# Carried-state matmuls in 64-row quadrants with a drain, states without zero blocks, stretches of two units and another opening, in a fused retention and ELU feed-forward kernel

## The chip, the cores and the metric

One of the eight cores of one Trainium2 chip runs the whole problem. The metric is the device time of one execution in microseconds (us). The core has five engines that run side by side, each through its own queue in order: TensorE (PE in the profile, its weight loads PEld), VectorE (DVE), ScalarE (ACT), GpSimd (POOL) and SyncE (SP), which here only issues transfers. Transfers run on 16 shared DMA engines.

## The reference

Multi-head retention over q, k, v of shape (8 batches, 8 heads, 576 positions, 64), then a feed-forward layer with an ELU-like function on the 4608 rows of 512:

```python
scores = scale * np.matmul(q, k.transpose(0, 1, 3, 2))
gamma = 1.0 - 2.0 ** (-5.0 - np.arange(H))
rel = pos[:, None] - pos[None, :]
Dmat = np.where(rel >= 0, gamma[:, None, None] ** rel[None, :, :], 0.0)
attn = np.matmul(scores * Dmat[None], v)

x = attn.transpose(0, 2, 1, 3).reshape(B * S, H * D)
h = x @ w_in                                   # 512 -> 2048
g = np.where(h > 0.0, h, np.exp(np.minimum(h, 0.0)) - 1.0)
out = g @ w_out                                # 2048 -> 512
```

## The kernel before

**Retention in chunks of 64.** The decay is split: q is multiplied by gamma to the power of its position and k by the inverse (`scaled`, L475), so that within a chunk of 64 positions a plain triangular mask is left, and all earlier chunks come in through a carried state, the running sum of k^T v per head. A *unit* n is a quarter of the first 512 positions and 8 heads of one batch: n = 4b + 2T + w, with batch b, T = 0 or 1 for the first or second 256 positions, and w for the first or last four heads. The last 64 positions of all batches form two *tails*, units 32 and 33 (t0, t1). Units 0 to 7 are laid out with even and odd positions apart; units 8 to 31 are "far" (`it.far`): positions in order, four chunks x = 0..3 each.

**What one far unit does.** SP loads q, k and v in two transfers each (L394). POOL scales q and k in four pieces and casts v (L475, L510). A DMA transpose (L562) makes qkT. PE then does four things for a unit, by these functions:

- `do_scores`: 16 matmuls of 64 rows by 64, one for each quadrant of the array in turn;
- `do_inter`: the carried states times the queries, into the output's PSUM bank. A state of two heads is kept as a 128x128 matrix with the two 64x64 blocks on the diagonal and zeros beside them, so one 128-row matmul serves both heads. It is 2 x 4 matmuls, and 2 x 3 where T = 0, for the first chunk of a batch has no state;
- `do_values`: 16 matmuls of 64 rows by 64, masked scores times v, added in the same bank;
- `do_state`: 16 matmuls of 64 rows by 64, k^T v of each chunk, into the other half of the same two banks.

`mask_step` (L837) masks the scores on DVE. `after_far` adds the four chunk states up on DVE (L801, L803), and its `emit_b` (L812) makes the block-diagonal form on POOL, from one 128x128 f32 sum to a 128x256 bf16 tile: three `s_mid` and one `s_end` per unit. `put_x` (L882) copies the output to xt on ACT or DVE.

**A stretch.** `stretch(prev, it)` puts one visit of PE to attention together: inter of the unit before, scores of this unit, values of the unit before, state of this unit. There is one stretch for each unit from 5 on, and a last one. It takes two of the six PSUM banks of class f (`SLOTS`), and the score tile sc. Units 0 to 4 are done in the opening by `early` and `early_out`.

**Feed-forward.** Blocks of rows go through `ffn1` (h = x w_in into a bank, exp on ACT L996, then ACT L1006 or DVE L1010, then DVE L1018 or L1020 gives g) and `ffn2` (g w_out into a bank, copied out on ACT L1054, stored by SP L1062). The first three batches make six narrow blocks of 256 rows, the others wide blocks of 512; the tails are a wide block of their own and come ahead of batch 7. F1 of one block alternates with F2 of the one before, in pieces of about 0.87 us on PE.

**Order.** Nothing is ordered by hand. All operations are given to `Plan`, each with a cost per engine that can do it, dependencies, a rank and buffers; `Plan.run` simulates the engines, the DMA queues and the buffers with these costs, always taking the ready operation of least rank, and the kernel emits every engine's instructions in the order that comes out. `FROM` holds the earliest times of the eight weight transfers (w_in then w_out, issued by POOL, L453 and L461), `ON` binds named operations to one engine, `RANKS` shifts named ranks, `FAR_LD`, `FAR_TR` and the `dma=` tuples hold what transfers are taken to cost. Up to 50 us the emitter also fills planned gaps of PE with matmuls on zeros (L268, L1178), so that its clock stays up.

The core of the stretch in the old kernel:

```python
if prev is not None:
    do_inter(prev, xkey)
if it is not None:
    do_scores(it)
if prev is not None:
    do_values(prev, xkey)
if it is not None and not it.tail:
    do_state(it, views)
```

Of the kernel before, what the change touches and what calls it, by code (L numbers as in the profile page):

```python
# [36 lines left out]
class Plan:  # L37
# [30 lines left out]
    def run(self, began):  # L68
# [58 lines left out]
        while len(order) < len(self.ops) or any(wire.values()) or events:  # L127
# [53 lines left out]
            for e, h in heads.items():  # L181
                h[1] -= step * rate[e]
                if h[1] < 1e-6:
                    wire[e].pop(0)
                    lanes[e] -= 1
                    heapq.heappush(events, (now + LEAVE, next(count), h[2]))
# [12 lines left out]
RANKS = {}  # L199
# [8 lines left out]
FROM = (8.96, 10.28, 13.13, 15.23, 17.0, 17.0, 17.44, 17.82)  # L208
ON = {'mid1': 'DVE', 'be2': 'DVE', 'md_1_0': 'ACT', 'xc1_2': 'DVE', 'cv0': 'DVE', 'md_1_1': 'ACT', 'cq12': 'DVE'}
DIRECT = True  # L210
FAR = 8
FAR_LD = 0.64
FAR_TR = 1.9
# [20 lines left out]
def kernel(  # L234
# [145 lines left out]
    def load_main(it, srcs="qkv"):  # L380
        n = it.n
        if not hasattr(it, "ld"):
            it.ld = {}
        for s in srcs:
            src = {"q": q, "k": k, "v": v}[s]
            key, cls = (("rv", n), "rv") if s == "v" else (("rq" + s, n), "rqk")

            away = (s, n) in AWAY

            if it.far:  # L390
                for e in range(2):
                    def emit_far(op, src=src, key=key, e=e):
                        i0 = 2 * P * it.T + e * P
                        pin(nc.sync.dma_start(tiles[key][:, :, e], src[it.b, 4 * it.w : 4 * it.w + 4, i0 : i0 + P, :].rearrange(  # L394
                            "h p d -> p h d")))

                    it.ld[s, e] = chain[0] = add(f"ld{s}{e}_{n}", {"SP": 0.52}, [], emit_far, len(plan.ops),
                                                 take=[] if e else [T(cls, key, [P, 4, 2, D], FP32)],
                                                 use=[key] if e else [], dma=(FAR_LD, 32), after=chain.get(0))
                continue  # L400

            def emit(op, src=src, key=key, away=away):
                dst = tiles[key].rearrange("p h e d -> p h (e d)")
                pin((nc.scalar if away else nc.sync).dma_start(  # L404
                    dst,
                    src[it.b, 4 * it.w : 4 * it.w + 4, 2 * P * it.T : 2 * P * (it.T + 1), :].rearrange(
                        "h (p e) d -> p h (e d)", e=2),
                ))

            take, use, held = [T(cls, key, [P, 4, 2, D], FP32)], [], []  # L410
            if s == "q" and n in HOLD:
                def emit_hold(op, key=key):
                    pin(nc.gpsimd.memset(tiles[key][:, 0, 0, :1], 0.0))

                held.append(add(f"hold{n}", {"POOL": 0.13}, [], emit_hold, -5, take=take))
                holds.append((held[0], HOLD[n]))
                take, use = [], [key]
            it.ld[s] = add(f"ld{s}{n}", {"ACT": 0.5} if away else {"SP": 0.46}, held, emit,
                           -10 ** 6 if away else len(plan.ops), take=take, use=use,
                           dma=(0.9 if n or s != "v" or away else 1.8, 32), after=None if away else chain.get(0))  # L420
            if away:
                it.ld[s].at = AWAY[s, n]
            else:
                chain[0] = it.ld[s]

    def load_tail(it):
# [3 lines left out]
        def load(name, cls, key, rows, src, b, first):  # L430
            def emit(op):
# [3 lines left out]
            chain[0] = add(name, {"SP": 0.46}, [], emit, len(plan.ops),  # L435
                           take=[T(cls, key, [P, H, D], FP32)] if first else [], use=[] if first else [key],
                           dma=(0.8, 32), after=chain.get(0))
# [8 lines left out]

    w_in_ld, w_out_ld = {}, {}

    def load_w_in(n0, n1, after):
# [5 lines left out]
        op = add(f"wi{n0}", {"POOL": 0.8}, [], emit, -1000, dma=(2.62 * (n1 - n0), 32 * (n1 - n0), 4.9), after=after)  # L455
# [3 lines left out]
    def load_w_out(n, after):  # L459
# [4 lines left out]
        w_out_ld[n] = add(f"wo{n}", {"POOL": 0.8}, [], emit, -1000, dma=(2.62, 32, 4.9), after=after)  # L464
# [102 lines left out]
    def prepare_tail(it):  # L567
# [3 lines left out]
        for m in range(2):  # L571
            for j in range(2):
# [14 lines left out]
                def emit_t(op, m=m, j=j):  # L587
# [5 lines left out]
                                     dma=(1.0, 32)))  # L593
# [27 lines left out]
    def do_scores(it):  # L621
        n = it.n
        sc = tiles["sc", n]
# [12 lines left out]
        if it.far:  # L636
            for x in range(4):
                for i in range(2):
                    r = slice(i * D, (i + 1) * D)
                    for c in range(2):  # L640
                        cs = slice(c * C, (c + 1) * C)
                        mm(sc[cs, i, x * C : (x + 1) * C], tt[r, 4 + x, cs], tt[r, x, cs], start=True, stop=True)
# [11 lines left out]
    def do_inter(it, xkey):  # L654
# [10 lines left out]
        if it.far:  # L665
            tt = tiles["qkT", n]
            for x in range(4):
# [4 lines left out]
                for hl in range(2):  # L672
                    acc((xkey, c), 0, 2, tiles[xkey, c][:, hl * P + e * C : hl * P + (e + 1) * C], s[:, hl],
                        tt[:, e * 2 + hl, c * C : (c + 1) * C])
# [114 lines left out]
    def after_far(it, st, views, bank_keys, prev):  # L789
# [3 lines left out]
        for x in range(4):  # L793
# [16 lines left out]

            def emit_b(op, key=key, out=out):
# [6 lines left out]
            blk = add(f"b{x}_{n}", {"POOL": 0.62, "DVE": (0.42, 1.5)}, [run], emit_b, it.rank + 3,  # L818
                      take=[T(name, out, [P, 2, P], BF16)], use=[key])
# [6 lines left out]
    def mask_step(it, sc):  # L826
        n = it.n
        def emit(op):
            if it.tail:
                pin(nc.vector.tensor_tensor(  # L830
                    tiles["pt", n].rearrange("p i h n -> p (i h n)").rearrange("p (x n) -> p x n", n=ST),
                    tiles["sc", n].rearrange("p i n -> p (i n)").rearrange("p (x n) -> p x n", n=ST),
# [3 lines left out]
            if it.far:  # L836
                pin(nc.vector.tensor_tensor(  # L837
                    far_pt(n).rearrange("p (i x) n -> p i x n", i=2),
                    tiles["sc", n][:, :, : 4 * C].rearrange("p i (x n) -> p i x n", n=C),
# [5 lines left out]
                tiles["sc", n].rearrange("p i (h n) -> p (i h) n", h=2),  # L845
# [4 lines left out]
                      take=[T("pt", ("pt", n), [P, 2, 2, 2 * P], BF16)], use=[("sc", n)], banks=[("sc", 0)])  # L850
# [40 lines left out]
    def cost_of(it, parts):  # L891
        t = 0.0
        if it.far:
            return ("i" in parts) * (0.27 + 0.06 * it.T) + 0.1 * sum(x in parts for x in "svt")
# [19 lines left out]
    def stretch(prev, it):  # L914

        xkey = ("x", it.n if it else "last")
        deps, use, take, cost = [], [], [], 0.22
        if prev is not None:
            deps += [prev.mask, *inter_deps(prev)]
            use += inter_uses(prev)  # L920
            cost += cost_of(prev, "iv")
        if it is not None:
            deps += it.turned + ([] if it.tail else [it.cv])
            take.append(T("sc", ("sc", it.n), [P, 2, 512], FP32))
            use += [("qkTt", it.n, m, j) for m in range(2) for j in range(2)] if it.tail else [("qkT", it.n), ("qkn", it.n), ("vn", it.n)]
            cost += cost_of(it, "st")
        views = [((xkey, c), 0, lambda c=c: tiles[xkey, c][:, 2 * P : 4 * P if it.far else 3 * P]) for c in range(2)]

        def emit(op):
            if prev is not None:  # L930
                do_inter(prev, xkey)
            if it is not None:
                do_scores(it)
            if prev is not None:
                do_values(prev, xkey)
            if it is not None and not it.tail:
                do_state(it, views)

        st = add(f"S{it.n if it else 'last'}", {"PE": cost}, deps, emit, (it or prev).rank - 4, take=take, use=use)
        reserve(st, [(xkey, c) for c in range(2)])  # L940
        if it is not None:
            mask_step(it, st)
            if not it.tail:
                after_state(it, st, views, [(xkey, 0), (xkey, 1)])
        if prev is not None:
            put_x(prev, xkey, st)

    def early(it):
        n = it.n
        sc = add(f"sc{n}", {"PE": 0.3}, it.turned, lambda op: do_scores(it), it.rank,  # L950
# [163 lines left out]
    for it in items[:EARLY]:  # L1114
        early(it)
        early_out(it)
    for n in range(4):
        load_w_in(n, n + 1, None)
    prev = None
    for it in items[EARLY:]:  # L1120
        stretch(prev, it)
        prev = it
    stretch(prev, None)
# [93 lines left out]
```

## Time and profile before

| what | value |
|---|---|
| median of 3 runs | 305.57 us (305.03 to 306.04) |
| the profiled execution's own time | 305.64 us |
| its span, first to last instruction | 303.9 us |
| mean granted TensorE clock | 1.000 |
| POOL, state blocks L812 | 72 s_mid 44.5 us busy, 24 s_end 15.6 us |
| PE, carried states of units | 160 s_mid matmuls 10.3 us, 32 s_end 3.8 us |
| HBM read, written | 36.70 MB, 9.44 MB |

The page is of one execution. Busy time of PE counts matmuls that overlap in the pipeline, so what one costs is read from the distance between starts. A group's mean in the page is the time from start to end of one matmul, 0.193 us for one of 64 columns, of which most lies beside its neighbours. Some matmul records are missing (a stretch can look one 512-column matmul longer than it is). "Waits" are idle times of an engine, put down to what came last. The 24 s_end operations of L812 are one per far unit.

### The profile page before, as it was taken

To read this page: it belongs to the slowest core of one execution; us is meant where nothing else is said; L and a number is where in the kernel's file an instruction comes from. 1 tells how busy PE (TensorE), PEld (TensorE's weight loads), DVE (VectorE), ACT (ScalarE), POOL (GpSimd) and SP (SyncE) were. 2 spreads that over 40 slices of the span, in tenths; PEclk is the share of its full clock that TensorE was granted. 3 is DMA by queue.
4 is the path that set the end of the run, shared out by engine and by line. 5 is a ranking of instruction groups with operands and counts; after the bars stand their busy time and mean duration, and the time that the engine had idled before them with its cause. 6 is when DMAs were issued, how large, how long until landed. Compare 5 with 4: busy or idle time off the path is not lost.

```text
span 303.9 us, 8654 instructions
## 1 busy us (share of the span) xinstructions
PE 291.6 (96%) x3378; PEld 169.6 (56%) x3418; DVE 214.2 (70%) x436; ACT 155.2 (51%) x305; POOL 178.4 (59%) x300
## 2 busy tenths in 40 slices
PE   8889999999999999999999999999997999999995
PEld 4768746767666754445554544545444544444444
DVE  5878935958877857996988897788871486666500
ACT  2439724748655546765855544445541583444311
POOL 5880389688989897889889889697532000000000
PEclk9999999999999999999999999999999999999999
DMA  7999998999899999989999999987667101011132
GB/s 206 270 206 210 235 303 218 173 218 187 194 193 232 214 185 204 206 193 183 193 188 224 204 186 199 204 169 171 137 130 168 37 2 36 35 36 37 43 97 71
DMA packets 142010, 50.13 MB, mean 165 GB/s; under 512 B 120720, under 2 KB 137488, under 8 KB 141968
## 3 DMA queue, kind: packets, MB, share of 16 engines
q1 hardware_dynamic: 137744, 45.37, 71.4%
q0 software_dynamic: 4224, 4.19, 8.3%
q8 instruction: 27, 0.44, 0.6%
q14 instruction: 15, 0.12, 0.1%
HBM read 36.70 MB, written 9.44 MB: 152 GB/s over the span
## 4 chain that ended last, share of the span: by engine, by line
PE 85%; DMA 6%; DVE 3%; issue 2%; SPq 1%; POOL 1%; ACT 1%; POOLq 0%; DVEq 0%; ACTq 0%
PE f L268 82%; PE sc L268 3%; DMA rv<-in_v_dram 3%; DMA rqk<-in_q_dram 2%; DMA rqt<-in_k_dram 1%; DVE em L1010 1%; DVE g L1020 1%; DMA qkTt<-qkt 1%; DVE g L1018 1%; SPq L404 1%; PE f L523 0%; ACT e L996 0%; POOL qkn L475 0%; POOL qkt L578 0%; DVE mid L803 0%
## 5 line engine op out<-in xcount | busy, mean ns | idle before, releaser
L268 PE MATMUL f<-xt,w_in_sb 128*128 128x256 bf16 (+1 forms) x755 | 139.8, 325 | 0.8 <-DVE xt L882 0.2
L268 PE MATMUL f<-w_out_sb,g 128*128 128x512 bf16 (+2 forms) x581 | 137.2, 367 | 3.4 <-issue 1.7
L996 ACT ACTIVATE e<-f 128x512 f32<-128x512 f32 x144 | 85.4, 597 | 77.7 <-PE f L268 73.5
L268 PEld LDWEIGHTS <-w_in_sb 128*128 128x128 bf16 x768 | 73.7, 98 | 52.0 <-DVE xt L882 0.5
L268 PEld LDWEIGHTS <-g 128*128 128x128 bf16 x608 | 56.5, 98 | 59.2 <-issue 1.0
L1010 DVE TENSOR_SCALAR em<-e 128x512 bf16<-128x512 f32 x88 | 49.2, 560 | 35.3 <-ACT e L996 34.7
L1020 DVE SCALAR_TENSOR_TENSOR g<-f,em 128x512 bf16<-128x512 f32 x88 | 60.4, 689 | 5.5 <-DVE em L1010 0.5
L812 POOL TENSOR_TENSOR s_mid<-mid,diag 128x256 bf16<-128x256 f32 x72 | 44.5, 630 | 15.1 <-DVE mid L803 9.5
L1018 DVE SCALAR_TENSOR_TENSOR g<-e,f 128x512 bf16<-128x512 f32 x56 | 37.6, 681 | 2.5 <-ACT f L1006 2.1
L1054 ACT COPY ot<-f 128x512 f32<-128x512 f32 (+2 forms) x37 | 20.8, 564 | 28.4 <-PE f L268 25.5
L475 POOL TENSOR_TENSOR qkn<-rqk,far_q 128x256 bf16<-128x256 f32 x48 | 31.0, 658 | 1.8 <-DMA rqk<-in_q_dram 1.6
L475 POOL TENSOR_TENSOR qkn<-rqk,far_k 128x256 bf16<-128x256 f32 x48 | 31.0, 660 | 0.0
L1006 ACT ACTIVATE f<-f 128x512 f32<-128x512 f32 x51 | 30.1, 594 | 0.0
L882 ACT CAST xt<-f 128x256 bf16<-128x256 f32 x52 | 18.1, 390 | 20.8 <-PE f L268 20.2
L510 POOL CAST vn<-rv 128x512 bf16<-128x512 f32 x28 | 18.2, 651 | 6.2 <-DMA rv<-in_v_dram 6.1
L837 DVE TENSOR_TENSOR pt<-sc,mask_t 128x512 bf16<-128x512 f32 x24 | 16.4, 681 | 5.9 <-PE sc L268 5.9
L803 DVE TENSOR_TENSOR mid<-f,mid 128x128 f32<-128x128 f32 x48 | 13.8, 288 | 3.5
L578 POOL TENSOR_TENSOR qkt<-rqt,gq 128x256 bf16<-128x256 f32 x16 | 10.1, 652 | 10.3 <-DMA rqt<-in_k_dram 10.2
L812 POOL TENSOR_TENSOR s_end<-end,diag 128x256 bf16<-128x256 f32 x24 | 15.6, 648 | 0.1
L475 POOL TENSOR_TENSOR qkn<-rqk,gq 128x256 bf16<-128x256 f32 x13 | 8.3, 648 | 12.0 <-DMA rqk<-in_q_dram 11.9
L843 DVE TENSOR_TENSOR pt<-sc,mask 128x1024 bf16<-128x1024 f32 x8 | 9.7, 1219 | 2.1 <-PE sc L268 2.0
L268 PE MATMUL sc<-qkT 64*64 64x64 bf16 (+1 forms) x512 | 11.0, 204 | 0.0
(83 smaller groups left out, 177.8 us busy)
## 6 DMA issues: line engine op xcount, KB each, us to landing
out_dram<-ot SPq DMA_DIRECT2D x26, 256.0 KB, 2.9
rqk<-in_q_dram SPq DMA_DIRECT2D x48, 128.0 KB, 3.4
rqk<-in_k_dram SPq DMA_DIRECT2D x48, 128.0 KB, 3.4
rv<-in_v_dram SPq DMA_DIRECT2D x48, 128.0 KB, 3.4
out_dram<-ot SPq DMA_DIRECT2D x19, 128.0 KB, 2.4
rqk<-in_q_dram SPq DMA_DIRECT2D x8, 256.0 KB, 6.1
rqk<-in_k_dram SPq DMA_DIRECT2D x8, 256.0 KB, 5.8
rv<-in_v_dram SPq DMA_DIRECT2D x8, 256.0 KB, 6.0
```

The source lines that it names most:

```text
L268: pin(nc.tensor.matmul(*a, **kw))
L475: pin(alu[op.eng].tensor_tensor(tiles[key][:, i, e], tiles[raw][:, :, e], g, ALU.mult))
L510: pin(copy[op.eng](tiles["vn", n], tiles["rv", n]))
L812: pin(alu[op.eng].tensor_tensor(tiles[out].rearrange("p h (j d) -> p h j d", j=2), tiles[key].unsqueeze(2).to_broadcast([P, 2, 2, D]), dia ...
L837: pin(nc.vector.tensor_tensor(far_pt(n).rearrange("p (i x) n -> p i x n", i=2), tiles["sc", n][:, :, : 4 * C].rearrange("p i (x n) -> p i ...
L882: pin(copy[op.eng](dst, src))
L996: pin(nc.scalar.activation(tiles[ekey], tiles[hkey], AF.Exp))
L1006: pin(nc.scalar.activation(ph, ph, AF.Relu))
L1010: pin(alu[op.eng].tensor_scalar_add(em, e, -1.0))
L1018: pin(nc.vector.scalar_tensor_tensor(g, e, -1.0, ph, ALU.add, ALU.min))
L1020: pin(nc.vector.scalar_tensor_tensor(g, ph, 0.0, tiles["em", blk, p], ALU.max, ALU.min))
L1054: pin(copy[op.eng](tiles[okey][:, :cols], tiles[pkey][:, :cols]))
```

## The change

1. `do_inter` of far units: the two heads' blocks are no longer one 128-row matmul. For each head i, 64 rows of the state and 64 rows of the queries go to 64 output partitions: twice as many matmuls, each 64x64 with 64 columns, in two quadrants of the array. Their states are kept as 128x64 (`[P, 2, D]`) tiles, made by a plain copy, `emit_c`, that POOL, ACT or DVE may do. The s_end of the T = 1 units, which the tails read, keep the block-diagonal form, and so do units 0 to 7.
2. A `nc.tensor.drain()` stands ahead of the values in each stretch that finishes a far unit.
3. `stretch` takes lists: from unit 20 on (`PAIR`), two units go through one stretch, with four output banks and one shared score tile (`it.sc`, `it.sc0`).
4. The opening and the costs: `FROM`, `ON`, `RANKS`, transfer costs and a new latency term for the weight transfers are set anew, and the planner orders everything afresh. `GATE` is off.

```diff
-RANKS = {}
+RANKS = {'F1_0_4': 5, 'ex_1_2': -8, 'ck01': -10, 'F1_0_1': -12, 'ck00': 6}
-FROM = (8.96, 10.28, 13.13, 15.23, 17.0, 17.0, 17.44, 17.82)
-ON = {'mid1': 'DVE', 'be2': 'DVE', 'md_1_0': 'ACT', 'xc1_2': 'DVE', 'cv0': 'DVE', 'md_1_1': 'ACT', 'cq12': 'DVE'}
+FROM = (9.61, 10.6, 13.6, 15.14, 15.57, 16.02, 17.92, 18.78)
+ON = {'mid1': 'DVE', 'be2': 'DVE', 'md_1_0': 'ACT', 'xc1_2': 'DVE', 'cv0': 'DVE', 'md_1_1': 'ACT', 'cq12': 'DVE', 'ck02': 'DVE', 'ck00': 'DVE', 'md_0_2': 'DVE', 'xc0_0': 'ACT', 'md_0_0': 'DVE', 'mid0': 'DVE', 'xc1_3': 'DVE'}
+GATE = False
+PAIR = 20
-FAR_LD = 0.64
-FAR_TR = 1.9
+FAR_LD = 0.62
+FAR_TR = 1.8
...
                 for hl in range(2):
-                    acc((xkey, c), 0, 2, tiles[xkey, c][:, hl * P + e * C : hl * P + (e + 1) * C], s[:, hl],
-                        tt[:, e * 2 + hl, c * C : (c + 1) * C])
+                    for i in range(2):
+                        r = slice(i * D, (i + 1) * D)
+                        acc((xkey, c), 0, i, tiles[xkey, c][r, hl * P + e * C : hl * P + (e + 1) * C], s[r, hl],
+                            tt[r, e * 2 + hl, c * C : (c + 1) * C])
...
+            def emit_c(op, key=key, out=out):
+                pin(copy[op.eng](tiles[out], tiles[key]))
+
...
-            blk = add(f"b{x}_{n}", {"POOL": 0.62, "DVE": (0.42, 1.5)}, [run], emit_b, it.rank + 3,
-                      take=[T(name, out, [P, 2, P], BF16)], use=[key])
+            if x < 3 or it.T == 0:
+                blk = add(f"b{x}_{n}", {"POOL": 0.27, "ACT": (0.28, 0.8), "DVE": (0.25, 1.0)}, [run], emit_c, it.rank + 3,
+                          take=[T(name, out, [P, 2, D], BF16)], use=[key])
+            else:
+                blk = add(f"b{x}_{n}", {"POOL": 0.62, "DVE": (0.42, 1.5)}, [run], emit_b, it.rank + 3,
+                          take=[T(name, out, [P, 2, P], BF16)], use=[key])
...
-            return ("i" in parts) * (0.27 + 0.06 * it.T) + 0.1 * sum(x in parts for x in "svt")
+            return ("i" in parts) * (0.18 + 0.03 * it.T) + 0.1 * sum(x in parts for x in "svt")
...
-    def stretch(prev, it):
+    def stretch(prevs, its):
...
         def emit(op):
-            if prev is not None:
-                do_inter(prev, xkey)
-            if it is not None:
+            for x, it in zip(xkeys, prevs):
+                do_inter(it, x)
+            for it in its:
                 do_scores(it)
-            if prev is not None:
-                do_values(prev, xkey)
-            if it is not None and not it.tail:
-                do_state(it, views)
+            if any(it.far for it in prevs):
+                pin(nc.tensor.drain())
+            for x, it in zip(xkeys, prevs):
+                do_values(it, x)
+            for v, it in zip(views, its):
+                if not it.tail:
+                    do_state(it, v)
...
-    prev = None
-    for it in items[EARLY:]:
-        stretch(prev, it)
-        prev = it
-    stretch(prev, None)
+    prev, left = [], items[EARLY:]
+    while prev or left:
+        now = left[: 2 if left and left[0].far and left[0].n >= PAIR else 1]
+        left = left[len(now) :]
+        stretch(prev, now)
+        prev = now
```

## The prediction

> **What bounds the kernel now.** I read the page first (busy rows and slices), then the matrix engine's waits, its timeline in single stretches, and the wait list of each queue.
>
> ```profile
> span 303.9 us, 8654 instructions
> PE 291.6 (96%) x3378; PEld 169.6 (56%) x3418; DVE 214.2 (70%) x436; ACT 155.2 (51%) x305; POOL 178.4 (59%) x300
> ...
> PE   8889999999999999999999999999997999999995
> ...
> POOL 5880389688989897889889889697532000000000
> PEclk9999999999999999999999999999999999999999
> DMA  7999998999899999989999999987667101011132
> ```
>
> PE is full from the third slice on, at the full clock, with one dent at slice 31. A busy PE is not a PE at its peak, so I also went by starts: the single starts in the trace of two feed-forward matmuls of 256 columns are 0.109 us apart and of 512 columns 0.216 us apart. By that the first layer's 384 narrow and 384 wide matmuls take 41.9 + 82.9 us and the second layer's (576 of full width, the last sixteen cut up) 124.4, 249.2 in all; attention and the opening fill the rest. So after about 20 us every microsecond that an attention stretch takes on PE is a microsecond of the end, and work on POOL, DVE, ACT and DMA counts only where PE runs out of ready work.
>
> Two stretches, PE alone (columns: start us, length us, engine, line, what, count):
>
> ```profile
> 85.64 0.22 PE L268 MATMUL f<-qkT,s_end 128*128 128x64 bf16 x2
> 85.69 0.34 PE L268 MATMUL f<-qkT,s_mid 128*128 128x64 bf16 x6
> 85.96 0.32 PE L268 MATMUL sc<-qkT 64*64 64x64 bf16 x16
> 86.11 0.30 PE L268 MATMUL f<-pt,vn 64*64 64x64 bf16 x16
> 86.24 0.30 PE L268 MATMUL f<-vn,qkn 64*64 64x64 bf16 x16
> 86.47 1.04 PE L268 MATMUL f<-w_out_sb,g 128*128 128x512 bf16 x3
> ...
> 92.56 0.34 PE L268 MATMUL f<-qkT,s_mid 128*128 128x64 bf16 x6
> 92.83 0.32 PE L268 MATMUL sc<-qkT 64*64 64x64 bf16 x16
> ```
>
> A stretch after a unit with T=1 takes 86.47 - 85.64 = 0.83 us, after T=0 (two matmuls fewer) 0.78. The 128-row matmuls start 0.029 us apart; between the last of them (85.840) and the first score (85.964) lie 0.124, so the turn from 128 to 64 rows costs 0.095. Sixteen 64-row matmuls take 0.13: they start in bursts of four, one for each quadrant of the array, a burst every 0.032. The turn back (86.355 to 86.473) costs 0.118 - 0.032 = 0.086.
>
> The one wait of size after the opening, first in the list of waits (us in total, times, longest), then in PE's timeline:
>
> ```profile
> PE sc L268 <- DMA qkTt<-qkt: 1.7, 1, 1.7
> ```
>
> ```profile
> 232.13 0.35 PE L268 MATMUL sc<-qkTt 64*64 64x64 bf16 x17
> 234.21 0.31 PE L268 MATMUL sc<-qkTt 64*64 64x64 bf16 x15 [1.73 <-DMA qkTt<-qkt]
> ```
>
> The second tail unit's last transpose lands at 234.2; PE stands from 232.28 to 234.21, 1.92 us by starts.
>
> **The change, part by part.** The sum is made against this execution, 305.64 us (span 303.9), 0.07 over the median of 305.57.
>
> *Carried-state matmuls.* 12 units x 8 and 12 x 6 matmuls of 128 rows (168) become 336 of 64 rows. Row i of the state feeds partitions i of the output, so only two of the four quadrants work: 16 matmuls are 8 bursts of two, 12 are 6. By the burst period that is 8 x 0.032 = 0.25 us where 8 x 0.029 = 0.23 stood, if a burst of two keeps 0.029 it is the same. The turn to 64 rows is not saved: it now lies ahead of these matmuls rather than behind. Cost 24 units x 0 to 0.02 = 0 to +0.4 us; I take +0.2.
>
> Four 64-row matmuls start within 0.01 us of each other here, so rows speak for overlap. The Trainium skill, "TensorEngine Tiling", section Performance Considerations, gives every matmul an overhead of about 60 cycles, so that one column costs as much as sixty, and this speaks against doubling their number. By that rule (an estimate, each added one at the 0.029 of 64 columns) the 168 would add 4.9 us; the bursts do not bear it out for four quadrants, and no run here shows two.
>
> *The drain.* The built program has 18 of them on PE: stretches 9 to 19 (11), the six of two units, and the first tail's. Each stands between scores and values, and queued behind it on PE are 16 to 32 value matmuls, the state matmuls and the next feed-forward tile; nothing else covers it. No drain inside the work is in the trace; the nearest rows are the end's, in the rows of the last source line (ns min/median/max) and in the timeline:
>
> ```profile
> L1212 PEldq DRAIN  x2: 13/604/1195, 299.5 to 303.5; - x2
> ```
>
> ```profile
> 298.82 1.84 PE L268 MATMUL f<-w_out_sb,g 128*128 128x128 bf16 x30
> ...
> 300.74 0.27 ACT L1054 COPY ot<-f 128x128 f32<-128x128 f32 x1 [0.63 <-PE f L268]
> ```
>
> The drain that starts at 299.51 takes 1.195 and ends at 300.705, 0.264 after the last matmul's start (300.441, 128 columns); with 64 columns (0.027 less) 0.237. Without it the first value follows the last score by 0.021 (86.090, 86.111). So 0.216 goes by, and then PE starts again with nothing preloaded: 0.02 more in the first burst, as behind a turn (85.964 to 86.016, not 0.032), and 0.02 to 0.05 to the first load, as behind a wait (ACT ends 17.73, PE starts 17.78). That makes 0.26 to 0.29. The low bound is the turn of the array, 0.095, which flushes it as well. I take 0.26, the row being of the same instruction: 18 x 0.26 = +4.7 us (1.7 to 5.2).
>
> *Stretches in pairs.* Units 20 to 31 take 6 stretches for 12. Each that goes saves two turns and the slow first burst, 0.095 + 0.086 + 0.02 = 0.20: -1.2 us.
>
> *States without zero blocks.* 84 POOL operations (L812: 72 at 0.612 us median, 12 s_end) become 84 copies of half the size, all on POOL. A copy is bounded by 0.16 (a quarter of the 128x512 cast at 0.65) and 0.61 (no gain). At 0.27 that is 84 x 0.35 = 29 us of POOL, off PE's path: worth nothing but earlier units.
>
> *What moves in time.* I counted the feed-forward matmuls ahead of each stretch in both programs. The second tail unit stood behind 184.4 us of them and stands behind 187.8. With 3.4 us more ahead and some 3.5 of longer stretches, PE comes to it at about 239 where the transpose lands at 234.2, so the wait goes: -1.9 us. Its supply is not later by POOL's or DMA's rows (above). The price if it is 5 us later: the 1.9 come back.
>
> Other stretches come earlier, up to 3.5 us in stretch 13 (16 x 0.109 + 8 x 0.216). There unit 13's transpose landed at 91.4 and the stretch began at 92.56; minus 3.5, plus four drains, it would begin at 90.1 and wait 1.3 us with the old supply. The supply hangs on POOL (0.9 busy) and a DMA share near 1.0 (195 to 220 GB/s), and SP stands behind POOL for its transposes (18.5 us in its list of waits), so POOL's relief, about 1.4 us a unit, should cover most. A stretch of two also wants four of the six PSUM banks at once, and stretch 24 sets block 5's first tile 1.7 us behind it, against 4 copies of 0.45 on ACT (1.8 and the hops). Bounds 0 and +2.5; I take +0.4.
>
> *The opening.* In the old one the last v of the first four units lands at 17.09, the first w_in piece at 17.75, and the feed-forward begins at 19.5. POOL's new order leaves the first two w_in issues behind the same loads (q1 at 7.41, k1 at 8.32, q2 at 10.06); the third goes behind one more state block (0.6 us), which gives the v of unit 3 a little of the wire. Ten more 128x128 matmuls on zeros (98 for 88, 10 x 0.056) fill PE and lie partly ahead of work. Bounds -0.5 and +1.0; I take 0. The w_out pieces go out up to 2 us earlier, which only shortens a wait that is not there.
>
> Sum: +0.2 + 4.7 - 1.2 - 1.9 + 0.4 + 0 = +2.2, so **307.8 us**.
>
> **The rivals.** What this measurement can tell from no change is about 0.3%, 0.9 us.
>
> *A, the forecast*, 307.8, own range 306.3 to 309.5. Chance 0.55.
>
> *B, not slower: the drain costs a flush only.* Place: the 18 drains. If PE's queue goes on taking instructions and only the array empties, each costs 0.10: 1.8 for 4.7, no waits, 305.64 + 1.8 + 0.1 - 1.2 - 1.9 = 304.4; with 0.3 from the opening 304.1. It decides below 0.11 a drain. For it: the turns, at 0.09. Against it: the end's drain, which held 0.26 after the last start. 0.17.
>
> *C: the two quadrants do not overlap.* The 168 added matmuls then take 0.029 each, +4.9 us: 312.7. Against it: all 64-row bursts of the trace overlap. 0.06. The page named above leans to this one.
>
> *D: the state matmuls halve.* If a quadrant takes its 64 columns in 0.015 us, 8 x 0.029 and 6 x 0.029 become half: 12 x 0.117 + 12 x 0.088 = 2.5 saved where A has 0.2 lost, 305.1. Against it: 0.029 at the full clock in every row. With a milder form, a drain near 0.19, 0.10.
>
> *E: PE waits for units or banks.* Supply stays as it is, and each of the six pairs and some earlier stretches wait about 0.8: 6 x 0.8 = 4.8, 312. For it: slacks of 1.2 to 5 us between landing and stretch in the old trace; against it: POOL's relief, and the later PE. It decides once POOL's copies take over 0.5. 0.12.
>
> **How the numbers follow.** The likeliest, A, gives 307.8. B's lower half (0.08) and the upper ends of C and E (0.12) are left out: 304.1 to 311.8. Faster by over 0.3% (under 304.7): B and a little, 0.18. Within: D and A's low edge, 0.17. Slower (over 306.5): the rest, 0.65.
>
> **What would show each step.** In the new timeline a stretch of one unit with a drain lasts 1.05 to 1.15 us from its first state matmul to the next feed-forward one; scores to values 0.25 to 0.3 apart in starts; 16 state matmuls 0.25 long; a stretch of two about 1.8 to 2.0. No wait on qkTt in PE's list. L821's copies near 0.27 on POOL. A drain under 0.15, state matmuls in 0.13, a feed-forward start before 19 us, or more than 2 us of new waits would prove me wrong.

## The result and the profile after

Over 6 runs the changed kernel took 307.97 us (median; 307.46 to 313.88), the kernel before 304.87 (303.30 to 306.04): a ratio of 1.0109, 95% interval [1.0071, 1.0147]. A second set of runs gave 307.49 against 304.33, 1.0122 [1.0082, 1.0162]. It is slower by about 3.1 us, 1.0%. The forecast was 307.8, with a chance of 0.65 for slower.

The first profiled execution of the changed kernel, 313.88 us, holds a stall near 55 us that the last section shows, so the profile shown is that of the second set (307.18 us, span 305.5). Its page:

```profile
span 305.5 us, 9034 instructions
...
PE 294.4 (96%) x3557; PEld 168.6 (55%) x3596; DVE 210.9 (69%) x440; ACT 154.8 (51%) x305; POOL 148.3 (49%) x296
...
PE   8999999999999999999999999999999999999996
...
POOL 3871289667856776774767758566342000000000
```

The dent of PE at slice 31 is gone, POOL is 30 us emptier (148.3 for 178.4), and yet the span is longer. The list of PE's waits (us in total, times, longest) has nothing left on qkTt or g:

```profile
PE f L270 <- issue: 2.8, 18, 0.2
PE f L270 <- DVE zero L275: 1.3, 1, 1.3
PE f L270 <- DVE xt L898: 0.4, 2, 0.2
PE sc L270 <- DVE pt L859: 0.3, 1, 0.3
```

The drains hardly show in this list. Of its 18 short waits on "issue" only five stand at values behind a drain, and the other 13 at second-layer matmuls, of which the old list has eleven. A matmul's record runs 0.193 us from its start, so by the records PE is idle for only 0.143 to 0.161 at a drain, and what a drain costs has to be read from starts. A stretch of one unit in PE's timeline, the one after a unit with T = 0 (start, length, line, what, count), to be laid beside the old 0.78 us from the first state matmul to the next feed-forward one:

```profile
67.11 0.38 PE L270 MATMUL f<-xt,w_in_sb 128*128 128x256 bf16 x2
67.42 0.31 PE L270 MATMUL f<-qkT,s_mid 64*64 64x64 bf16 x8
67.55 0.22 PE L270 MATMUL sc<-qkT 64*64 64x64 bf16 x2
67.57 0.20 PE L270 MATMUL f<-qkT,s_mid 64*64 64x64 bf16 x2
67.60 0.20 PE L270 MATMUL sc<-qkT 64*64 64x64 bf16 x2
67.60 0.20 PE L270 MATMUL f<-qkT,s_mid 64*64 64x64 bf16 x2
67.63 0.30 PE L270 MATMUL sc<-qkT 64*64 64x64 bf16 x12
68.07 0.32 PE L270 MATMUL f<-pt,vn 64*64 64x64 bf16 x16
68.21 0.30 PE L270 MATMUL f<-vn,qkn 64*64 64x64 bf16 x16
68.45 0.28 PE L270 MATMUL f<-xt,w_in_sb 128*128 128x256 bf16 x1
```

It takes 68.448 - 67.424 = 1.02 us, and the turn to 64 rows now lies ahead of it (single starts: 0.202 from the last feed-forward matmul to the first of the stretch, where two feed-forward ones stand 0.109 apart), so 1.12 in all. Between the last score's start, 67.733, and the first value's, 68.069, nothing starts for 0.336; the old kernel had 0.022. That hole is the drain. Stretches after T = 1 take 1.18 with the turn (0.84 before), those of two units 1.72 and 1.83 to 1.85 (without the 512-column matmul whose record is missing behind some of them).

At the tail, what was a stall of 1.92 us is a plain stretch of 1.20 (it was 3.14):

```profile
238.98 0.63 PE L270 MATMUL f<-qkTt,s_end 128*128 128x64 bf16 x16
239.54 0.45 PE L270 MATMUL sc<-qkTt 64*64 64x64 bf16 x32
239.81 0.44 PE L270 MATMUL f<-pt,vt 64*64 64x64 bf16 x32
```

### The profile page after: what moved, and what is told of

The parts are those of the page before. It is cut to its first block, busy times and chain, and to the rows that moved or that the text cites. A ratio compares the mean times of both kernels' runs of the same rounds, so it can differ in the third digit from the quotient of the medians.

```text
span 312.2 us, 9034 instructions
## 1 busy us (share of the span) xinstructions
PE 297.4 (95%) x3557; PEld 169.5 (54%) x3596; DVE 217.4 (70%) x440; ACT 154.8 (50%) x305; POOL 148.3 (48%) x296
## 4 chain that ended last, share of the span: by engine, by line
PE 91%; DVE 5%; issue 2%; ACT 0%; DVEq 0%; ACTq 0%
PE f L270 88%; PE sc L270 3%; DVE em L1035 2%; DVE pt L859 1%; PE f L530 1%; DVE qkn L482 1%; DVE xt L898 0%; DVE qkT L536 0%; DVE end L764 0%; PE f L1205 0%; DVE g L1045 0%; DVE s_mid L786 0%; DVE s_end L772 0%; ACT e L1021 0%; DVE mid L755 0%
## 5 line engine op out<-in xcount | busy, mean ns | idle before, releaser
L270 PEld LDWEIGHTS <-w_in_sb 128*128 128x128 bf16 x768 | 74.7, 99 | 58.4 <-issue 3.9
L1035 DVE TENSOR_SCALAR em<-e 128x512 bf16<-128x512 f32 x93 | 53.9, 581 | 37.5 <-ACT e L1021 36.5
L1045 DVE SCALAR_TENSOR_TENSOR g<-f,em 128x512 bf16<-128x512 f32 x93 | 63.8, 689 | 5.7 <-DVE em L1035 0.5
L821 POOL CAST s_mid<-mid 128x128 bf16<-128x128 f32 x72 | 21.5, 305 | 36.7 <-DVE mid L812 20.5
L1043 DVE SCALAR_TENSOR_TENSOR g<-e,f 128x512 bf16<-128x512 f32 x51 | 34.3, 681 | 3.4 <-ACT f L1031 2.8
L898 ACT CAST xt<-f 128x256 bf16<-128x256 f32 x57 | 19.0, 393 | 33.2 <-PE f L270 33.2
L1031 ACT ACTIVATE f<-f 128x512 f32<-128x512 f32 x46 | 27.2, 595 | 0.0
L482 POOL TENSOR_TENSOR qkn<-rqk,gq 128x256 bf16<-128x256 f32 x12 | 7.2, 612 | 13.8 <-DMA rqk<-in_q_dram 13.8
L270 PE MATMUL f<-pt,vn 64*64 64x64 bf16 (+1 forms) x512 | 9.8, 202 | 2.8 <-issue 1.1
```

Source lines behind the costliest of these rows:

```text
L270: pin(nc.tensor.matmul(*a, **kw))
L482: pin(alu[op.eng].tensor_tensor(tiles[key][:, i, e], tiles[raw][:, :, e], g, ALU.mult))
L821: pin(copy[op.eng](tiles[out], tiles[key]))
L898: pin(copy[op.eng](dst, src))
L1031: pin(nc.scalar.activation(ph, ph, AF.Relu))
L1035: pin(alu[op.eng].tensor_scalar_add(em, e, -1.0))
```

## The experiments

How the traces are compared. Executions differ by over a microsecond in the opening alone. In all these kernels but one the same feed-forward work (208 matmuls of 256 columns and 84 of 512, 40.8 us) stands ahead of stretch 9, the first of those that carry drains in the changed kernel; in old_opening it is eight of 256 columns, 0.87 us, less. So each span is cut at that stretch's first matmul, and the part behind it is compared. Two profiles of one and the same kernel differ there by 1.42 us (before), 0.67 (full_rows and full_rows_2) and 0.02 (the changed kernel), so a small difference counts only where single stretches show it:

```
kernel              start of stretch 9   from there to the end   median us
before                    67.56               236.37             304.3 to 305.1
before_again              69.98               234.95
changed (after_again)     67.42               238.06             307.49
before_drains             68.49               241.40             310.71
full_rows                 68.33               234.24             303.55
full_rows_2               67.27               233.57             303.81
no_pairs                  67.98               241.19             310.89
full_rows_no_pairs        67.06               234.17             304.09
pairs_alone               66.78               237.00             307.31
old_opening               66.34               240.34             309.75
two_drains                67.83               239.61             310.02
drain_first               68.54               237.88             308.09
zero_blocks               70.60               238.53             309.71
```

**after_again: the changed kernel once more.** No edit.

> The changed kernel itself, to have an undisturbed profile of it. Theory (drain 0.26 us each, state matmuls as before, pairs save 0.2 each, tail wait of 1.9 us gone): 307 to 308.5 us; a stretch of one unit 1.02 to 1.10 us, of two 1.85 to 2.0, no wait on qkTt. Rival (the loss sits in new waits of PE, not in the stretches): the stretches last under 0.95, and PE's list of waits holds over 2 us that the old kernel has not.

307.49 us (307.07 to 308.34); the profile shown above is this one. The time is as expected, and so is the missing wait on qkTt. A stretch of one unit takes 1.02 or 1.09 us without the turn, and one of two, at 1.72 to 1.85 with it, is a little shorter than expected. The rival, new waits of PE, is out.

**before_drains: the drain alone, in the old kernel.**

```diff
+            if prev is not None and prev.far:
+                pin(nc.tensor.drain())
             if prev is not None:
                 do_values(prev, xkey)
```

> The kernel before with one drain ahead of the values in each of the 24 stretches that finish a far unit, nothing else changed. Theory: each adds 0.24 to 0.27 us to its stretch, 24 x 0.26 = 6.2, less the 1.9 us that PE waits for the second tail's transpose, which the later PE no longer does: +4.0 to +4.6 us against the kernel before. Rival (a drain is a flush of the array, 0.1): +2.4 - 1.9 = +0.5 us.

310.71 us, ratio 1.0229 [1.0170, 1.0288], 6.4 over before in the medians of that set: more than expected; behind stretch 9 the profiles differ by 5.0. A stretch with a drain:

```profile
68.49 0.34 PE L268 MATMUL f<-qkT,s_mid 128*128 128x64 bf16 x6
68.76 0.32 PE L268 MATMUL sc<-qkT 64*64 64x64 bf16 x16
69.21 0.32 PE L268 MATMUL f<-pt,vn 64*64 64x64 bf16 x16
```

The stretches take 1.091 for 0.778 (T = 0) and 1.149 for 0.836, so 0.313 for a drain where I had 0.26: the hole between scores and values is 0.320 for 0.022 (0.293 in six of the 24), and the values' first burst is slow (0.015). Twenty-four of these are 7.4 us, and the wait at the second tail, 1.93, went in return, for PE came there 8.1 us later and the last transpose only 5.6. Rival B of the prediction, a mere flush at 0.10, is out.

**full_rows: everything of the change but quadrants and drains.** States are 128-row blocks with zeros again, no drains.

```diff
-                    for i in range(2):
-                        r = slice(i * D, (i + 1) * D)
-                        acc((xkey, c), 0, i, tiles[xkey, c][r, ...], s[r, hl], tt[r, ...])
+                    acc((xkey, c), 0, 2, tiles[xkey, c][:, ...], s[:, hl], tt[:, ...])
...
-            if any(it.far for it in prevs):
-                pin(nc.tensor.drain())
```

> The changed kernel with the carried states as block-diagonal 128-row matmuls again and so without drains (POOL makes the blocks, planner costs of that part as before); stretches of two and the new opening stay. Theory: the 18 drains (4.7 us) go and the state matmuls change by 0 to 0.4: about 4.5 us under the changed kernel, near 303 us, 1 to 2.5 under the kernel before, by six stretches saved (1.2) and the tail wait (up to 1.9). Rival (the loss is in pairs or the opening): within 1 us of the changed kernel.

> Leaves the result as it is; states as 128-row blocks without drains, with the change's stretches of two and its opening, once more beside the next two. If the looks so far hold: 303.0 to 304.0 us, 0.3 to 1.3 under before. Waits of PE on DVE's and POOL's mid and s_mid of 0.2 to 0.4 each again, no wait of the last stretch on qkTt.

303.55 us, ratio 0.9999 [0.9961, 1.0037], and in the second set 303.81, 0.9985 [0.9952, 1.0019]. The whole loss is in the parts taken out: 3.9 us come back. But the kernel is only level with before, not 1 to 2.5 under it. By the lengths of the stretches the quadrants and drains cost 6.1 us (26.6 for 20.5, summed from stretch 9 on, without waits); behind stretch 9 only 3.8 to 4.5 came back. Most of the rest went to waits that shorter stretches laid bare: in full_rows_2 feed-forward matmuls at 136.0, 154.6 and 165.3 us start 0.17, 0.26 and 0.40 late, and two behind stretches 0.16 and 0.28 (DVE's mid and g stand in PE's list there), 1.3 us in all. Another 0.2 lies behind the last matmul (3.23 us from its start to the end, for 3.02), and 0.1 is not placed.

**no_pairs: one unit to a stretch throughout.** `PAIR = 99`, the rest as changed.

> The changed kernel with one unit in every stretch, so 24 drains instead of 18 and six more stretches. Theory: 6 x (0.26 + 0.20) = 2.8 us over the changed kernel, less what the pairs cost by waits (0 to 1): +1.8 to +2.8. Rival (pairs make PE wait for units or banks): 0 to 3 us under the changed kernel.

310.89 us, ratio 1.0235 [1.0198, 1.0271]; 3.4 over the changed kernel in the medians, 3.14 behind stretch 9, a little above what was expected. Its 24 drains at 0.33 are 7.9 us, the changed kernel's 18 are 5.8 (next section), which is 2.1 of it; the other 1.0 is what six stretches of two save, a little under the 1.2 of the prediction.

**full_rows_no_pairs: of the change only the new opening and transfer costs.** Both edits above.

> As full_rows_2, with one unit to a stretch throughout: what is left of the change is its opening. Theory 1 (stretches of two are worth about 0.7 us by the stretches' own lengths, and the opening nothing): 0.5 to 1.0 us over full_rows_2, if the last stretch is again free of its wait; with the wait of 1.9 us back at qkTt, 2.4 to 2.9 over. Rival (the stretches of two also cause the small waits on mid and s_mid that full_rows had): these waits are gone and the time is that of full_rows_2 or less.

304.09 us, 0.9996 [0.9959, 1.0033]. Behind stretch 9 it is 0.60 longer than full_rows_2, which is theory 1's side, but 0.06 shorter than full_rows, a profile of the same kernel; the medians, 0.3 apart, can't tell either. What a stretch of two saves is plain in single stretches, 1.405 us for 2 x 0.778. The wait at the second tail is gone here too, with no drain in the program:

```profile
230.40 0.63 PE L270 MATMUL f<-qkTt,s_end 128*128 128x64 bf16 x16
230.96 0.45 PE L270 MATMUL sc<-qkTt 64*64 64x64 bf16 x32
231.23 0.44 PE L270 MATMUL f<-pt,vt 64*64 64x64 bf16 x32
```

PE comes at 230.4, earlier than the 231.6 of the old kernel, and finds everything there: the last transpose for the tails landed at 227.5 (single records), where it was 234.2 before. So the new plan of transfers is enough by itself to take that wait away; later arrival, on which I had counted, is another way to the same end (before_drains). In the changed kernel it is by lateness: there the last transpose lands at 234.9 and PE comes at 239.0.

**pairs_alone: the stretches of two in the old kernel**, old opening, no drains.

> Before's kernel with nothing but the stretches of two of units 20 to 31; opening, states and transfers' costs as before, no drains. Theory 1 (stretches of two save 0.7 us, the new opening is worth nothing): 0.5 to 0.9 us under before if the wait at qkTt stays at its length plus what is saved earlier, which it then takes back (then 0 to 0.3 under), and as full_rows_2. Rival (the new opening carried the gain or the loss): differs from full_rows_2 by over 0.7 us in either direction, with the difference standing before 20 us in the trace.

307.31 us, ratio 1.0086 [1.0052, 1.0120]: slower than before by 2.8 in the medians (its profile, at 305.49, is of the shortest of 12 runs and behind stretch 9 only 0.6 longer than before's), and 3.5 over full_rows_2, which differs by the opening and the transfer costs alone. That is the rival's size, but it doesn't stand before 20 us; it stands in the stretches of two, and in the old order's waits on g near 132 us (0.87) and at the tail (1.09), which came along:

```profile
177.88 0.34 PE L270 MATMUL f<-qkT,s_mid 128*128 128x64 bf16 x6
179.23 0.34 PE L270 MATMUL f<-qkT,s_mid 128*128 128x64 bf16 x6 [1.01 <-DVE g L1041]
...
210.93 0.34 PE L270 MATMUL f<-qkT,s_mid 128*128 128x64 bf16 x6 [0.44 <-DVE g L1041]
```

PE does the first unit's six state matmuls and then stands, until DVE has read a bank with g: the second unit's output banks are not free. By lengths the two stretches are 1.17 and 0.71 over those of full_rows_2. The stretch of two wants four banks at once, and the order of that plan does not have them ready. In full_rows_2 the same twelve run through:

```profile
151.17 0.51 PE L270 MATMUL f<-qkT,s_mid 128*128 128x64 bf16 x12
151.61 0.45 PE L270 MATMUL sc<-qkT 64*64 64x64 bf16 x32
```

**old_opening: the changed kernel with before's opening and transfer costs.**

> The changed kernel with before's opening and transfer costs; drains, 64-row state matmuls, copies and stretches of two stay. Theory 1 (the wait at the second tail went because PE comes there later, by drains and order, and the opening is worth nothing): 307 to 308.3 us, no wait on qkTt over 0.3. Rival (the new opening and transfer costs took that wait away and keep the units early): a wait on qkTt of 0.9 to 1.9 and waits on g of about 1 again, as in pairs_alone, 309 to 311 us.

309.75 us, ratio 1.0174 [1.0114, 1.0235]. Each held against before's median of its own set, it is 1.5 over the changed kernel (4.67 for 3.16). Behind stretch 9 the difference is 2.28, but there 0.87 of it is feed-forward work that this plan still has before it, so it is 1.4. The rival is nearer. The tail waits again, though for less than it forecast:

```profile
239.21 0.34 PE L270 MATMUL sc<-qkTt 64*64 64x64 bf16 x17
240.01 0.32 PE L270 MATMUL sc<-qkTt 64*64 64x64 bf16 x15 [0.46 <-DMA qkTt<-qkt]
```

The stretch is 0.66 longer for it (1.863 for 1.204). Two first-layer matmuls, at 164.9 and 189.5, start 0.26 late each, where PE's weight load waits for DVE's mid, and 0.2 is not placed.

**two_drains: a second drain right behind each.**

> The changed kernel with a second drain right behind each of its 18. Theory 1 (a drain costs 0.32 us because the matmuls in flight have to complete, and what is left, a restart, is small): the second finds nothing in flight and adds 0.01 to 0.06 each, 0.2 to 1.1 us in all. Rival (each drain has a fixed price that doesn't depend on what is in flight): 0.15 to 0.3 each, 2.7 to 5.4 us in all.

310.02 us, ratio 1.0170 [1.0114, 1.0226]; 1.55 over the changed kernel behind stretch 9. In the stretches scores and values lie 0.416 apart for 0.336, so 0.080 for each second drain, 1.44 in all (one stretch holds 0.10 more). The second drain itself is recorded with 13 ns. The 0.08 lies between the two theories, nearer to theory 1's 0.06 than to the 0.15 of its rival. If the first drain has the same part, then some 0.08 of its 0.33 is fixed, and 0.25 is waiting for matmuls in flight and starting again.

**drain_first: the drain ahead of the scores.**

```diff
-            for it in its:
-                do_scores(it)
             if any(it.far for it in prevs):
                 pin(nc.tensor.drain())
+            for it in its:
+                do_scores(it)
```

> The changed kernel with the drain moved from behind the scores to ahead of them, right behind the state matmuls; 18 drains as before. Theory 1 (a drain costs the last matmuls' way through the array, 0.24, and a restart, 0.08, whatever they are): 0.30 to 0.34 from the last state matmul to the first score, 0.02 from the last score to the first value, and the time of the changed kernel within 0.6 us (306.9 to 308.1). Rival (the scores that start beside the last state matmuls in idle quadrants gain something that the drain then takes away): scores no longer overlap, 0.03 to 0.06 more in each of 18 stretches, 0.5 to 1.1 us over the changed kernel.

308.09 us, ratio 1.0114 [1.0046, 1.0181]; behind stretch 9 0.18 under the changed kernel. The hole has moved and is nearly as long:

```profile
68.54 0.38 PE L270 MATMUL f<-qkT,s_mid 64*64 64x64 bf16 x12
69.02 0.32 PE L270 MATMUL sc<-qkT 64*64 64x64 bf16 x16
69.17 0.30 PE L270 MATMUL f<-pt,vn 64*64 64x64 bf16 x16
```

From the last state matmul's start, 68.719, to the first score's are 0.303. Theory 1 holds: whichever matmuls are last, the way through is waited for. The few scores that begin among the state matmuls when they are next in order (67.55 to 67.60 in the changed kernel's stretch) are worth nothing: a stretch of one unit takes 0.991 here for 1.024. The quadrants without any drain were not run, nor with another instruction in its place.

**zero_blocks: the quadrants read from zero blocks.** The blocks are made on POOL as before, drains stay.

```diff
-acc((xkey, c), 0, i, tiles[xkey, c][r, ...], s[r, hl], tt[r, ...])
+acc((xkey, c), 0, i, tiles[xkey, c][r, ...], s[r, hl, r], tt[r, ...])
...
-            if x < 3 or it.T == 0:
+            if False:
```

> The changed kernel with all carried states made as 128x256 blocks with zeros on POOL again; PE's 64-row matmuls read the 64x64 corners of them, drains and stretches of two as they were. Theory 1 (POOL's relief of 72 x 0.3 us is off the path): the changed kernel's time within 0.7 us (306.8 to 308.2), POOL 175 to 180 us busy, no new wait over 0.5 us. Rival (that relief paid for PE's earlier stretches): waits of PE on s_mid, mid or qkT of 0.2 to 0.8 in several stretches, 1 to 3 us over the changed kernel.

309.71 us (308.38 to 313.84), ratio 1.0162 [1.0081, 1.0242], over the 306.8 to 308.2 expected; POOL is 176.8 us busy. Behind stretch 9 it is 0.47 over the changed kernel, and no wait over 0.5 is there: a first-layer matmul at 162.9 starts 0.26 late, two holes at drains (170.7, 210.8) are 0.13 and 0.06 longer. Ahead of stretch 9 this profile has a stall of 3.21 us (last section) that lengthens its 309.1 of span. Of the runs, 308.38 and 308.58 lie 3.3 and 3.5 over before's median of their set, where the changed kernel lies 3.2 over that of its own. POOL's relief is worth up to some 0.5 us: small, as forecast, and not told from nothing.

**before_again: a second profile of the old kernel.**

> The kernel before, for a second profile. Theory 1 (its first profile had an accidental 0.9 us wait of PE near 132 us on ACT's vn, and the wait on qkTt is a standing one): from the start of unit 9's stretch to the end of the span 235.0 to 235.6 where the first had 236.3, with 1.5 to 2.0 on qkTt and no wait of 0.9 near 132. Rival (both stand in every execution): 236.0 to 236.6 with both waits.

306.75 us. From stretch 9 to the end 234.95, and neither theory as it stands. The wait at the second tail is 0.97 by starts where it was 1.93: PE came 2.4 us later there, after a longer opening, and the last transpose was issued only 1.45 later (233.14 for 231.69). So that wait absorbs a part of what the opening loses, here 1.0 of 2.4 us. The other wait I had put near 132 us on vn. It is on g, and it stands in both executions (0.70 and 0.71 in the lists of waits). PE's timeline of the first:

```profile
131.12 1.90 PE L268 MATMUL f<-xt,w_in_sb 128*128 128x512 bf16 x7
133.73 0.59 PE L268 MATMUL f<-w_out_sb,g 128*128 128x512 bf16 x2 [0.70 <-DVE g L1020]
```

The last first-layer matmul starts at 132.64, the first second-layer one at 133.73: 1.08 for 0.216, so 0.87 lost. The changed kernel's plan doesn't have it. Between stretch 9 and the second tail's, the two executions of the old kernel take 164.005 and 164.007 us: that part is repeated to a few ns.

## Why the prediction was right, and where it was not

The number was right (307.8 for 307.5 to 308.0), the direction and the mechanism too: the drains are the loss. By its own steps, as far as the runs separate them, between the two profiles:

```
step                  predicted    measured     from
state matmuls           +0.2         +0.3       turn to last score 0.402 for 0.394, 0.466 for 0.452
18 drains               +4.7         +5.8       0.33 each in eleven stretches of one unit, 0.30 to 0.34 in the seven others
stretches of two        -1.2         -1.0       lengths without waits, 20.5 in full_rows_2 for 21.5 in before; no_pairs
wait at second tail     -1.9         -1.9       3.14 to 1.20
new waits               +0.4          0         none over 0.2 behind the opening
wait on g at 133 us      (none)      -0.9       before, before_again
behind last matmul       (none)      -0.5       3.02 us from its start to the end, for 3.50
opening                  0           -0.1       starts of stretch 9
sum                     +2.2         +1.7
```

The two profiled executions are 1.54 apart (307.18 and 305.64), so 0.14 is open. The 0.5 behind the last matmul is no gain of the change: before_again has 3.04 there too.

**The step that was mis-sized is the drain.** The prediction took it from the end's drain, 0.237 after the last matmul's start, and 0.02 to 0.05 for the restart. In the trace the drain ends 0.277 after the last score's start (67.563 + 0.447 = 68.010, against 67.733), the first value starts 0.059 after that, and from there to the feed-forward it is 0.379 for 0.362, for the first burst is slow: 0.353 less the old 0.022, 0.33. So the drain ends 0.04 later than assumed and PE starts again more slowly. In stretches of two the hole is 0.344 and the values and states behind it take 0.664 for 0.687, so 0.30; in before_drains it is 0.31. The row of the drains (ns min/median/max, first and last start):

```profile
L955 PEldq DRAIN  x18: 337/447/447, 67.6 to 223.5; - x18
```

Its 447 ns are not its price, for it begins while scores are still being issued; the hole between starts is. The upper bound I gave, 0.29, was too low for every drain, and the hole of 0.25 to 0.3 that was to show the step measured 0.336.

**The state matmuls** came out as worked out: sixteen go in 8 bursts of two, 0.25 us, and from the turn to the last score a stretch of one unit is 0.008 to 0.014 longer. Rival C, two quadrants that don't overlap, would have added 0.2 a unit. The Trainium skill's 60 cycles for every matmul ("TensorEngine Tiling (Array Packing)", Performance Considerations) don't show here: the two of a burst start 3.5 ns apart. D, halving, is out by the same row.

**The wait that I missed.** I called the wait on qkTt the only one of size after the opening; the list of waits of the old profile has a line on g of 0.7 too, and I took it for one of the opening. That it went in the new order (0.87) hides, with the 0.4 of new waits that didn't come, that attention was put 1.4 too cheap (5.1 by the measured lines, 3.7 by mine).

**The base.** The medians differ by 3.1 where 2.2 were forecast and the two profiles show 1.5, because 305.64 lay 0.8 above the median of before in the result and 0.6 to 1.3 above those of the later sets (305.08, 304.49, 304.33). Part of that is its wait of 1.93, which before_again halves, and the 0.5 at its end. That the number came out to 0.3 us is in good part luck: drains too cheap, waits that went unforeseen, and a base that was too long offset each other.

**The tail's wait** went for the reason given (PE at 239.0 as forecast, transpose at 234.9 for 234.2). That PE came at 239.0 was two errors again: the stretches ahead cost 5.0 more, not 3.5, and the wait on g was gone. **The opening:** seven profiles with the new one start stretch 9 at 67.06 to 68.54, mean 67.78 (two more, with the stall of the last section, at 70.60 and 74.09), and five with the old one at 66.34 to 69.98, mean 68.0 with old_opening's 0.87 us of work added: no gain clear of the scatter. A feed-forward start before 19 us, which the prediction named as a sign of being wrong, did come (18.88), but it is no such sign: the start lies at 18.61 to 19.99 in the nine profiles with the new opening, and at 18.71 to 20.62 in the five with the old one. What the opening's edits do bring lies behind it, in the order of all that follows, and depends on the kernel: pairs_alone and old_opening are the worse for lacking them by 3.5 (over full_rows_2) and 1.5 us, and the old kernel alone gains nothing that the medians show (full_rows_no_pairs). That is a part of the change that the prediction put at nothing, though the planner's costs set everything afresh. **POOL's copies** take 0.293 in the median (303 ns mean), for 0.27:

```profile
L821 POOL CAST s_mid<-mid x72: 284/293/533, 64.8 to 211.0; 128x128 bf16<-128x128 f32 x72
```

**Rival E** (waits for units or banks) did not come about in the changed kernel, but pairs_alone shows it was real: with another order, a stretch of two stands 1.01 us for its banks. At stretch 13, where the prediction weighed a wait of 1.3, PE came at 90.31 (90.1 forecast) and the unit's transpose had landed at 89.56, 1.85 us earlier than in the old kernel.

No version tried beats both kernels: full_rows and full_rows_no_pairs are level with before within 0.5%, and before's waits at the tail and on g, 2.8 us in its profile, went in them without a gain that the medians show.

## What to carry to other kernels

Price a drain on the matrix engine by the hole in starts around it, here 0.31 to 0.33 us each, and multiply by how often it stands on the path: a split into quadrants that needs a drain has to save more than that per visit, and here it saved nothing on that engine. Relief of an engine that isn't the bound (30 us of POOL) bought at most some 0.5 us. Before cutting traces at a common point, count the work ahead of it: in old_opening 0.87 us of an apparent loss was only work done later. Before costing what a new order brings, list every standing wait of the old one: two of them (1.9 and 0.9 us) went with the order, not with the edit that looked responsible.

## What the runs showed of the hardware that was not expected

**A drain costs something with nothing in flight:** 0.080 us for the second of two, though it is recorded with 13 ns, and 0.33 for one with matmuls in flight. The records give one 64-column matmul 0.193 from start to end. By the Trainium skill, "TensorE: Matmul & The Clock Gate", Single matmul latency, an estimate is (398 + 64) / 2.4 = 192.5 ns, with its formula for a matmul on the full array. That is the same figure, but the ends of matmuls in these records are modelled, so it is no measurement. The drain ended 0.277 after the last start, 0.085 later than that latency.

**Matmuls start out of program order.** In the stretch at 67.42 two scores start at 67.546, ahead of state matmuls (67.572) that the program issues before them; by the program the state matmuls use only two of the four quadrants. The same page of the Trainium skill, Part 3, Packing small matmuls, has matmuls in strict order of start and end; by these records starts are not, where different quadrants are concerned.

**An operation on DVE took 5.2 us beside a run of POOL.** In zero_blocks' profile, DVE's and POOL's timelines:

```profile
51.24 5.19 DVE L1035 TENSOR_SCALAR em<-e 128x512 bf16<-128x512 f32 x1 [1.82 <-ACT e L1021]
```

```profile
50.98 1.19 POOL L482 TENSOR_TENSOR qkn<-rqk,far_q 128x256 bf16<-128x256 f32 x2
52.12 1.19 POOL L482 TENSOR_TENSOR qkn<-rqk,far_k 128x256 bf16<-128x256 f32 x2
53.25 0.62 POOL L517 CAST vn<-rv 128x512 bf16<-128x512 f32 x1
53.82 1.19 POOL L482 TENSOR_TENSOR qkn<-rqk,far_q 128x256 bf16<-128x256 f32 x2
54.96 1.19 POOL L482 TENSOR_TENSOR qkn<-rqk,far_k 128x256 bf16<-128x256 f32 x2
```

The operation (median 0.43) ends at 56.43, 0.3 after POOL's run of operations without a gap, and PE stands 3.21 us for its g. The first profile of the changed kernel has the same: the operation, at 51.89, is 5.16 us long and again ends 0.3 after POOL's run. There PE stands 3.19 us, its granted clock is 0.70 and 0.62 in the two stretches of 5 us from 55 on, and stretch 9 begins 6.67 us later than in the profile shown above, which is what made it 313.88; behind stretch 9 the two are alike to 0.02. In the profile shown above the same operation, at 51.44, took 0.53 beside the same run of POOL. The Trainium skill, "SBUF — State Buffer", Who interferes with whom, has a port pair that DVE, in some of its modes, shares with POOL, and that the one that issues first holds for a whole instruction. That would explain one operation of 0.6 waited for, as in several cases of 0.87 to 0.90, but not that DVE waits through eight of them; no trace here shows which mode the operation ran in. That POOL held DVE off is argued from where the two operations ended, not shown, and what decides between 0.53 and 5.2 is open. Both stalls came with the new opening, in two of its nine profiles.
